# A new order for the repeating stage of an attention kernel: two first mixes together, scores late, the second mixes apart

## The chip, the cores and the metric

One core of a Trainium2 chip runs one program. The metric is the time of one execution on the device in microseconds (us). Five engines work beside each other, each through its own instructions in order: TensorE (PE in the profile, with its weight loads as PEld), VectorE (DVE), ScalarE (ACT), GpSimd (POOL), and SyncE (SP), which here issues the DMA transfers.

## The reference

Three parts follow each other: an attention whose heads are mixed before and after the softmax, an ELU layer, and a layer of eight experts with routing. The change lies in the first part alone. With batch 4, 12 heads, 448 positions and head width 64:

```python
scores = (1 / sqrt(64)) * q @ k.transpose(0, 1, 3, 2)
scores = einsum('bhij,hg->bgij', scores, w_pre)        # first mix
scores = scores - max(scores, axis=-1, keepdims=True)
attn = exp(scores)
attn = attn / (sum(attn, axis=-1, keepdims=True) + 1e-09)
attn = einsum('bhij,hg->bgij', attn, w_post)           # second mix
out = attn @ v                                         # values
# then: ELU layer (1792x768 by 768x2048 and back), and the experts
```

## The kernel before, in words

The queries of a batch are cut into four tiles: three of 120 rows and one of 88. A tile's scores are computed for all heads, laid out anew by DMA so that 10 rows by 12 heads fill the partitions, mixed, put through the softmax, mixed again and multiplied with the values. A block is 10 query rows (the last two of an 88-row tile are 4 rows), a pair is two blocks, and a unit is two pairs; the last unit of an 88-row tile has one pair. There are 16 tiles of three units, so 48 **periods**, `for n in range(NP)`. A period works on four things at once, in a software pipeline written out by hand:

- the **first mix** (`mix_pre`, tile `c`, L200) of the pairs of unit n: 8 products of 64 rows by 64 columns on TensorE a pair; then maxima (`top`, DVE L208), exponentials with their sums (`softmax`, ACT L217), reciprocals (`norm`, DVE L224 and L225) and the scaled mixing weights `kr` (POOL L229);
- the **second mix** (`mix_post`, tile `f`, L243) of the pairs of unit n-1: 64 products, 64 by 64, into two PSUM buffers, which are all there are of this kind (`ps_f`, 2), and two copies out of them into `at` (L248);
- the **scores** (`qk`, L159) of a unit five periods ahead: 12 products of 64 rows by 120 (or 88) columns, and copies to `s` on ACT (L163) and DVE (L164); their queries are split into a high part (ACT L146) and a low part (DVE L147), and at the start of a batch the keys likewise (ACT L138, POOL L139);
- the **values** (`av`, tile `xp`, L264) of a tile whose second mix is finished: 24 products of 128 rows by 64 columns and 8 of 64 by 64, a copy (DVE L273) and a store.

SP issues the new layout (`relayout`, L192), the loads and the stores, in program order. In the last five periods `next(mix)` puts pieces of the ELU layer's preparation between these steps, at four places of a period.

The order of the body is the order of the calls. Before the change it is: first mix of pair 0, second mix of old pair 0, first mix of pair 1, second mix of old pair 1, scores, values. A second mix is followed at once by one copy on ACT and one on DVE. `ps_w`, five buffers, holds the results of first mixes and scores.

Of the kernel before, what the change touches and what calls it, by code (L numbers as in the profile page):

```python
# [8 lines left out]
FP32 = mybir.dt.float32  # L9
# [3 lines left out]
ACTF = mybir.ActivationFunctionType  # L13
ALU = mybir.AluOpType
# [4 lines left out]
B, H, S, D = 4, 12, 448, 64  # L19
# [57 lines left out]
def attention(tc, q, k, v, w_pre, w_post, xT, mix):  # L77
# [12 lines left out]
    with ExitStack() as ctx, ExitStack() as mixing, ExitStack() as scoring:  # L90
        pool = lambda name, bufs, ctx=ctx, **kw: ctx.enter_context(tc.tile_pool(name=name, bufs=bufs, **kw))
        at_p = pool("a_at", 2)
        e_p = pool("a_e", 6)
        st_p = pool("a_st", 4)
        const = pool("a_const", 1)
        v_p = pool("a_v", 1)
# [44 lines left out]
        def split_q(T, u):  # L141

            n = ROWS[tiles[T][1]][1]
            t = qt[T, u] = q_p.tile([128, 2, 2, 120], FP32R, tag="q", name="qq")
            raw = raw_q[T][:, 2 * u:2 * u + 2, :n]
            nc.scalar.copy(out=t[:, 0, :, :n], in_=raw)  # L146
            nc.vector.tensor_tensor(out=t[:, 1, :, :n], in0=raw, in1=t[:, 0, :, :n], op=ALU.subtract)  # L147

        def qk(T, p):

# [24 lines left out]
        dr, cs, tops, sms, es, ks = {}, {}, {}, {}, {}, {}  # L175

        d_all = [d_p.tile([128, S], FP32, name=f"d{i}") for i in range(ND)]
        n_d = [0]
# [16 lines left out]
        def mix_pre(U):  # L195
            pss = [ps_w.tile([128, 512], FP32, tag="w", name="c") for _ in range(2)]
            d = dr.pop(U)
            for j in range(2):
                for z, ps in enumerate(pss):
                    nc.tensor.matmul(out=ps[j * UP:(j + 1) * UP, :S], lhsT=kpre_up[UP:UP + HP, :] if z else kpre_low,  # L200
                                     rhs=d[z, j])
            cs[U] = [ps[:, :S] for ps in pss]

        def top(U):
            tops[U] = []
            for c in cs[U]:
                t = st_p.tile([128, 1], FP32, tag="nmx", name="nmx")
                nc.vector.tensor_reduce(out=t, in_=c, op=ALU.max, axis=AX.X, negate=True)  # L208
                tops[U].append(t)

        def softmax(U):

            sms[U] = st_p.tile([128, 2], FP32, tag="sm", name="sm")
            es[U] = []
            for i, (c, t) in enumerate(zip(cs.pop(U), tops.pop(U))):
                e = e_p.tile([128, S], FP32, tag="e", name="e")
                nc.scalar.activation(out=e, in_=c, func=ACTF.Exp, bias=t, accum_out=sms[U][:, i:i + 1])  # L217
                es[U].append(e)

        def norm(U):  # L220

            sm = sms.pop(U)
            rs = st_p.tile([128, 2], FP32, tag="rs", name="rs")
            nc.vector.tensor_scalar(out=rs, in0=sm, scalar1=1e-9, scalar2=None, op0=ALU.add)  # L224
            nc.vector.reciprocal(out=rs, in_=rs)  # L225
            ks[U] = []
            for i in range(2):
                kr = e_p.tile([128, HP], FP32, tag="kr", name="kr")
                nc.gpsimd.tensor_scalar(out=kr, in0=kposts[i], scalar1=rs[:, i:i + 1], scalar2=None, op0=ALU.mult)  # L229
                ks[U].append(kr)  # L230

        def mix_post(U):

# [127 lines left out]
        for n in range(NP):  # L361
            cur, old = units[n], units[n - 1] if n else ()
            new = units[n + 1] if n + 1 < NP else ()
            T, u = when(n + 5)
            T1, u1 = when(n + 6)
            T2, u2 = when(n + 7)
            for U in new[1:]:
                relayout(U)
            store()
            if n == NP - 5:  # L370
                scoring.close()
            late = n >= NP - 5
# [11 lines left out]
            for i in range(2):  # L384
# [12 lines left out]
                if i == 0:  # L397
                    softmax(cur[i])
                if i == 1 and T < len(tiles):
                    scores = [qk(T, 2 * u), qk(T, 2 * u + 1)]  # L400
                if late:
                    next(mix)
            norm(cur[0])
            for f in scores:
                f()
            for U in cur[1:]:
                norm(U)
            if T1 < len(tiles):
                split_q(T1, u1)
            if n >= 3:  # L410
                av(n // 3 - 1, n % 3)()
            if T1 < len(tiles) and tiles[T1][1] == 0:
                split_k(tiles[T1][0], 2 * u1, nc.gpsimd)
                split_k(tiles[T1][0], 2 * u1 + 1, nc.gpsimd)
            if late:
                next(mix)
        mixing.close()
# [893 lines left out]
```

## Time and profile before

| | us |
|---|---|
| median of 3 runs | 1040.65 (1037.43 to 1047.15) |
| the profiled execution | 1035.86 |
| its span | 1034.1 |
| attention, its steady periods (52 to 330 us of the span) | 278 |

The busy time of an engine is the union of its instructions. Starts of products on TensorE are recorded; their ends are modelled, so the distance from the start of one group to the start of the next is the better measure of a group. The row of a timeline that merges several instructions has the start of the first.

### The profile page before, as it was taken

The numbers are of one execution on the slowest core, as the hardware profiler recorded it, in microseconds if no ns is written. First come the engines' busy times: TensorE is split into PE (matmuls) and PEld (weight loads), VectorE is DVE, ScalarE is ACT, GpSimd is POOL, SyncE is SP. The second block draws the span as 40 slices with busy tenths as digits, with TensorE's granted clock in tenths as the row PEclk, the third lists the DMA queues.
The fourth block names the chain that finished last, engine by engine and source line by source line (L and its number), as shares of the span: only waits on it lengthen the run. The fifth ranks groups of instructions, "written<-read, shape, count | busy, mean of one in ns | idle before, by whom it ended". The sixth has DMA issues, their size and how long they took to land. (4 is left out here: it accounts for less than half of the span.)

```text
span 1034.1 us, 30182 instructions
## 1 busy us (share of the span) xinstructions
PE 993.6 (96%) x12226; PEld 874.0 (85%) x12226; DVE 768.2 (74%) x1589; ACT 531.8 (51%) x1077; POOL 228.3 (22%) x295
## 2 busy tenths in 40 slices
PE   7899999999999899999999999999999999899997
PEld 4577777777777688999999998999999998798987
DVE  6678788788788788767666576868686848999963
ACT  5557567567666565444544453121212107788861
POOL 2134224223322312222333200101000003312001
PEclk9899999999999999999999999999999999999999
DMA  5555566466555685545665469633343387999800
GB/s 166 198 174 145 166 217 181 150 205 192 156 185 179 179 248 190 158 163 173 222 216 194 170 211 311 205 92 123 93 122 96 99 310 264 394 395 399 340 9 34
DMA packets 134219, 199.69 MB, mean 193 GB/s; under 512 B 35860, under 2 KB 101400, under 8 KB 133821
## 3 DMA queue, kind: packets, MB, share of 16 engines
q1 hardware_dynamic: 131933, 191.27, 56.2%
q0 software_dynamic: 2144, 6.46, 1.6%
q8 instruction: 97, 1.59, 0.7%
q14 instruction: 45, 0.37, 0.1%
HBM read 122.47 MB, written 37.65 MB: 155 GB/s over the span
## 5 line engine op out<-in xcount | busy, mean ns | idle before, releaser
L855 PE MATMUL o<-w,gh 128*128 128x384 f32 (+2 forms) x1344 | 238.9, 337 | 2.2 <-ACT w L460 1.6
L855 PEld LDWEIGHTS o<-w,gh 128*128 128x128 f32 x1344 | 231.9, 188 | 5.3 <-ACT w L460 2.0
L582 PE MATMUL h<-xh,w 128*128 128x448 f32 x1152 | 234.5, 365 | 0.0
L582 PEld LDWEIGHTS h<-xh,w 128*128 128x128 f32 x1152 | 216.1, 188 | 17.6 <-issue 0.2
L243 PEld LDWEIGHTS f<-kr,e 64*64 64x64 f32 x5888 | 121.5, 137 | 51.0 <-issue 34.0
L229 POOL TENSOR_SCALAR kr<-kpost,rs 128x60 f32<-128x60 f32 x184 | 80.9, 454 | 252.4 <-DVE rs L225 227.8
L243 PE MATMUL f<-kr,e 64*64 64x60 f32 x5888 | 121.5, 223 | 9.6 <-issue 3.6
L745 DVE SCALAR_TENSOR_TENSOR junk<-x,wrow 128x768 f32<-128x768 f32 x117 | 111.8, 955 | 18.1 <-ACT x L885 12.8
L1023 DVE TENSOR_TENSOR wlo<-w1t,whi 128x1536 fp32r<-128x1536 f32 x64 | 110.9, 1751 | 14.3 <-ACT whi L1021 13.9
L208 DVE TENSOR_REDUCE nmx<-c 128x1 f32<-128x448 f32 x184 | 106.2, 619 | 19.5 <-PE c L200 19.2
L217 ACT ACTIVATE e<-c,nmx 128x448 f32<-128x448 f32 x184 | 114.4, 639 | 2.1 <-DVE nmx L208 2.1
L248 ACT COPY at<-f 128x480 f32<-128x480 f32 (+1 forms) x92 | 52.1, 566 | 114.2 <-PE f L243 114.2
L497 POOL TENSOR_TENSOR wf<-a,p 128x768 f32<-128x768 f32 x32 | 66.6, 2082 | 178.1 <-DVE p L495 141.1
L1021 ACT CAST whi<-w1t 128x1536 fp32r<-128x1536 f32 x64 | 93.9, 1482 | 20.6 <-PE ph L1050 9.9
L200 PE MATMUL c<-d,kpre_up 60*64 60x448 f32 x368 | 94.1, 565 | 1.6 <-ACT s L163 1.6
L264 PEld LDWEIGHTS xp<-at,v 128*64 128x64 f32 (+1 forms) x1536 | 74.0, 135 | 24.7 <-issue 14.1
L264 PE MATMUL xp<-at,v 128*64 128x120 f32 (+3 forms) x1536 | 91.1, 265 | 3.6 <-DVE rs L225 1.8
L200 PE MATMUL c<-d,kpre_low 64*64 64x448 f32 x368 | 91.5, 552 | 2.9 <-DMA d<-s 2.9
L159 PE MATMUL qk<-k,qq 64*120 64x448 f32 (+1 forms) x576 | 80.0, 400 | 8.1 <-ACT k L138 5.1
L730 ACT CAST gh<-gr 128x512 fp32r<-128x512 f32 x56 | 35.0, 625 | 98.7 <-PE o L855 38.8
L159 PEld LDWEIGHTS qk<-k,qq 64*120 64x120 f32 (+1 forms) x576 | 52.6, 182 | 23.5 <-ACT k L138 5.9
L248 DVE COPY at<-f 128x480 f32<-128x480 f32 (+1 forms) x92 | 58.8, 640 | 13.9 <-PE f L243 9.7
(177 smaller groups left out, 1251.8 us busy)
## 6 DMA issues: line engine op xcount, KB each, us to landing
w1t<-in_moe_w_dram SPq DMA_DIRECT2D x64, 768.0 KB
d<-s SPq DMA_DIRECT2D x176, 210.0 KB
gT<-g SPq DMA_DIRECT2D x64, 224.0 KB
f<-in_moe_w_in_dram SPq DMA_DIRECT2D x16, 768.0 KB
f<-in_moe_w_out_dram SPq DMA_DIRECT2D x16, 768.0 KB
gr<-gT SPq DMA_DIRECT2D x48, 256.0 KB
rk<-in_k_dram SPq DMA_DIRECT2D x24, 224.0 KB
xr<-xT SPq DMA_DIRECT2D x24, 224.0 KB
```

The lines of the kernel that those rows point to most:

```text
L159: nc.tensor.matmul(out=ps[:n, :S], lhsT=qt[T, p // 2][rows, a, p % 2, :n], rhs=kt[b, p][rows, z, :], start=(i == 0), stop=(i == 2))
L200: nc.tensor.matmul(out=ps[j * UP:(j + 1) * UP, :S], lhsT=kpre_up[UP:UP + HP, :] if z else kpre_low, rhs=d[z, j])
L208: nc.vector.tensor_reduce(out=t, in_=c, op=ALU.max, axis=AX.X, negate=True)
L217: nc.scalar.activation(out=e, in_=c, func=ACTF.Exp, bias=t, accum_out=sms[U][:, i:i + 1])
L243: nc.tensor.matmul(out=ps[to, c // 2, :, z, :], lhsT=e[rows, keys], rhs=kr[rows, :])
L248: copy(out=to[:, :, r + j * m:r + (j + 1) * m], in_=at[:, :, first:first + m])
L264: nc.tensor.matmul(out=ps[z * 64:(z + 1) * 64, i, :n], lhsT=t[:, z, jc % t.shape[2], :], rhs=att[T][:t.shape[0], jc, 2 * p + z, :n], start ...
L582: nc.tensor.matmul(out=ps, lhsT=w[:, a, kk, :], rhs=xs[tb, kk][:, z, :], start=(kk == 0 and a + z == 0), stop=(kk == NK - 1 and a == 1))
L745: nc.vector.scalar_tensor_tensor(out=t[:, o:o + n], in0=x2, scalar=1.0, in1=w, op0=ALU.mult, op1=ALU.mult, accum_out=lg[:, e:e + 1])
L855: mm = nc.tensor.matmul(out=po[c][:, :cols[c].stop - cols[c].start], lhsT=gs[i][fc // GC][:, a, fc % GC, :], rhs=wo[fc][:, z, cols[c]], st ...
L1021: nc.scalar.copy(out=hi, in_=t)
L1023: nc.vector.tensor_tensor(out=lo, in0=t, in1=hi, op=ALU.subtract)
```

## The change

The body of the period is written in another order: both first mixes, the second mix of old pair 0, the values (of the tile that was finished a period earlier than before, `n - 1` in place of `n`), all scores, the second mix of old pair 1. The split of the queries moves from one period ahead into the period of the scores: its high part on ACT before the first mixes' exponentials, its low part on DVE behind the four maxima. `norm` is called once for both pairs, on one tile of four sums. The two copies of the last second mix both go to ACT. The split of the keys is spread over the period, the weights' pool gets a seventh buffer, and the four `next(mix)` of a late period stand at other places.

```diff
-        e_p = pool("a_e", 6)
+        e_p = pool("a_e", 7)
...
-        def norm(U):
-
-            sm = sms.pop(U)
-            rs = st_p.tile([128, 2], FP32, tag="rs", name="rs")
...
+        def norm(Us):
+
+            k = 2 * len(Us)
+            sm = sms.pop(0)
+            es_now.clear()
+            rs = st_p.tile([128, 4], FP32, tag="rs", name="rs")
+            nc.vector.tensor_scalar(out=rs[:, :k], in0=sm[:, :k], scalar1=1e-9, scalar2=None, op0=ALU.add)
+            nc.vector.reciprocal(out=rs[:, :k], in_=rs[:, :k])
...
-            if late:
-                next(mix)
...
-            scores = []
-            for i in range(2):
-                if i < len(cur):
-                    mix_pre(cur[i])
+            if n and T < len(tiles):
+                high_q(T, u)
+            for i, U in enumerate(cur):
+                mix_pre(U)
                 if i == 0 and n + 2 < NP:
                     relayout(units[n + 2][0])
-                moves = mix_post(old[i]) if i < len(old) else []
-                if i < len(cur):
-                    top(cur[i])
-                    if i == 1:
-                        softmax(cur[i])
-                if moves:
-                    moves[1](nc.scalar.copy)
-                    moves[0](nc.vector.tensor_copy)
-                if i == 0:
-                    softmax(cur[i])
-                if i == 1 and T < len(tiles):
-                    scores = [qk(T, 2 * u), qk(T, 2 * u + 1)]
-                if late:
-                    next(mix)
-            norm(cur[0])
+            for U in cur:
+                top(U)
+            if n and T < len(tiles):
+                low_q(T, u)
+            softmax(cur[0])
+            moves, scores = [mix_post(U) for U in old[:1]], []
+            weighted = [av((n - 1) // 3 - 1, (n - 1) % 3)] if n >= 4 else []
+            if T < len(tiles):
+                scores.append(qk(T, 2 * u))
+            for U in cur[1:]:
+                softmax(U)
+            if late:
+                next(mix)
+            for m in moves:
+                m[1](nc.scalar.copy)
+                m[0](nc.vector.tensor_copy)
+            keys = T1 < len(tiles) and tiles[T1][1] == 0
+            if keys:
+                split_k(tiles[T1][0], 2 * u1, nc.gpsimd)
+            if late:
+                next(mix)
+            norm(cur)
+            for f in weighted:
+                f()
+            if T < len(tiles):
+                scores.append(qk(T, 2 * u + 1))
             for f in scores:
                 f()
-            for U in cur[1:]:
-                norm(U)
-            if T1 < len(tiles):
-                split_q(T1, u1)
-            if n >= 3:
+            if keys:
+                split_k(tiles[T1][0], 2 * u1 + 1, nc.gpsimd)
+            moves = [mix_post(U) for U in old[1:]]
+            if late:
+                next(mix)
+            for m in moves:
+                m[1](nc.scalar.copy)
+                m[0](nc.scalar.copy)
+            if n == NP - 1:
                 av(n // 3 - 1, n % 3)()
...
```

A full period on TensorE, before (`c` first mix, `f` second mix, `qk` scores, `xp` values; a second mix is 32 products in the program, 64 on the engine):

```order
L200 MATMUL c<-d_154,kpre_low 64x448
L200 MATMUL c<-d_154,kpre_up 64x448
L200 MATMUL c<-d_155,kpre_low 64x448
L200 MATMUL c<-d_155,kpre_up 64x448
L243 MATMUL f<-kr,e 64x12x5 x32
L200 MATMUL c<-d_156,kpre_low 64x448
L200 MATMUL c<-d_156,kpre_up 64x448
L200 MATMUL c<-d_157,kpre_low 64x448
L200 MATMUL c<-d_157,kpre_up 64x448
L243 MATMUL f<-kr,e 64x12x5 x32
L159 MATMUL qk<-k,qq 120x448 x12
L264 MATMUL xp<-at,v 64x120 x16
```

The same period with the change:

```order
L208 MATMUL c<-d_154,kpre_low 64x448
L208 MATMUL c<-d_154,kpre_up 64x448
L208 MATMUL c<-d_155,kpre_low 64x448
L208 MATMUL c<-d_155,kpre_up 64x448
L208 MATMUL c<-d_156,kpre_low 64x448
L208 MATMUL c<-d_156,kpre_up 64x448
L208 MATMUL c<-d_157,kpre_low 64x448
L208 MATMUL c<-d_157,kpre_up 64x448
L264 MATMUL f<-kr,e 64x12x5 x32
L285 MATMUL xp<-at,v 64x120 x16
L167 MATMUL qk<-k,qq 120x448 x12
L264 MATMUL f<-kr,e 64x12x5 x32
```

The two second mixes no longer have only a first mix between them: values and scores stand there now, and two first mixes behind the last one.

A full period on ScalarE with the change (`e` exponentials, `at` copies of the second mix, `s` copies of the scores, `qq` high part of the queries):

```order
L145 CAST qq<-rq 128x240
L229 ACTIVATE e,sm<-c,nmx 128x448 x4
L269 COPY at<-f 128x48x10
L171 ACTIVATE s<-qk 120x448 x2
L269 COPY at<-f 128x48x10 x2
```

Before, the queue had one copy `at` ahead of the four exponentials, one behind them, then the scores and last the queries' cast; now the cast is first and the two copies of the second mix stand together at the end, with the next period's cast behind them.

## Rows read from the trace of the kernel before

**Rows 1.** Windows: length, busy PE, PEld, DVE, ACT, POOL (count), granted clock, DMA, GB/s.
```profile
52.00:330.00 278.00, 270.35 (x7124) 208.03 (x7118) 222.49 (x531) 184.31 (x509) 85.30 (x169) 1.00 0.57 178
```

**Rows 2.** Waits, 52 to 330 us: who waited for whom, us, times, longest.
```profile
PEld f L243 <- issue: 26.5, 33, 1.2
...
PEld xp L264 <- issue: 13.1, 55, 0.3
...
PEld xp L264 <- ACT at L248: 4.6, 9, 0.6
```

**Rows 3.** Timeline of TensorE's products, one full period: start, us, what.
```profile
146.23 0.59 PE L200 MATMUL c<-d,kpre_up 60*64 60x448 f32 x1
...
147.03 1.24 PE L243 MATMUL f<-kr,e 64*64 64x60 f32 x63
148.05 0.54 PE L200 MATMUL c<-d,kpre_up 60*64 60x448 f32 x1
...
148.43 0.54 PE L200 MATMUL c<-d,kpre_up 60*64 60x448 f32 x1
...
149.09 1.30 PE L243 MATMUL f<-kr,e 64*64 64x60 f32 x64
150.32 1.45 PE L159 MATMUL qk<-k,qq 64*88 64x448 f32 x12
151.70 1.90 PE L264 MATMUL xp<-at,v 128*64 128x120 f32 x29
153.34 0.59 PE L200 MATMUL c<-d,kpre_up 60*64 60x448 f32 x1
...
153.44 0.27 PE L264 MATMUL xp<-at,v 64*64 64x120 f32 x2
```

**Rows 4.** Timeline of TensorE, first and last full period's first product (39 periods apart).
```profile
52.51 0.59 PE L200 MATMUL c<-d,kpre_up 60*64 60x448 f32 x1
...
330.40 0.59 PE L200 MATMUL c<-d,kpre_up 60*64 60x448 f32 x1
```

**Rows 5.** Timeline of ScalarE in the same period.
```profile
148.38 0.57 ACT L248 COPY at<-f 128x480 f32<-128x480 f32 x1 [1.71 <-PE f L243]
148.84 0.63 ACT L217 ACTIVATE e<-c,nmx 128x448 f32<-128x448 f32 x1
...
151.28 0.59 ACT L248 COPY at<-f 128x480 f32<-128x480 f32 x1
151.73 0.99 ACT L163 ACTIVATE s<-qk 88x448 f32<-88x448 f32 x2
```

**Rows 6.** Groups by form, 52 to 330 us: busy us, mean ns, idle before.
```profile
L139 POOL TENSOR_TENSOR k<-rk,k 128x448 fp32r<-128x448 f32 x18 | 20.0, 1133 | 0.0
```

**Rows 7.** Timeline of TensorE, a period behind a unit of one pair.
```profile
281.63 0.59 PE L200 MATMUL c<-d,kpre_up 60*64 60x448 f32 x1
...
286.05 0.86 PE L159 MATMUL qk<-k,qq 64*120 64x448 f32 x5 [0.19 <-ACT e L217]
286.84 1.50 PE L264 MATMUL xp<-at,v 128*64 128x88 f32 x29
288.11 0.59 PE L200 MATMUL c<-d,kpre_up 60*64 60x448 f32 x1
```

**Rows 8.** Timeline of TensorE in the last periods, without scores.
```profile
333.26 1.30 PE L243 MATMUL f<-kr,e 64*64 64x60 f32 x64
334.49 1.90 PE L264 MATMUL xp<-at,v 128*64 128x120 f32 x29
...
364.03 2.01 PE L264 MATMUL xp<-at,v 128*64 128x120 f32 x32
365.97 3.92 PE L582 MATMUL h<-xh,w 128*128 128x448 f32 x18
```

**Rows 9.** Timeline of SP and ScalarE: load of the ELU layer's first weights, its first use.
```profile
331.92 0.35 SPq L474 DMA_DIRECT2D f<-in_moe_w_in_dram  x1
...
338.24 0.89 ACT L485 ACTIVATE a<-f 128x768 f32<-128x768 f32 x1 [2.20 <-DMA d<-s]
```

More of the change, by code (lines that the diff above doesn't have):

```diff
@@ L139, in split_k, with high_q, low_q, split_q @@
             eng.tensor_tensor(out=t[:, 1], in0=raw, in1=t[:, 0], op=ALU.subtract)
-        def split_q(T, u):
+        def high_q(T, u):
             n = ROWS[tiles[T][1]][1]
             t = qt[T, u] = q_p.tile([128, 2, 2, 120], FP32R, tag="q", name="qq")
-            raw = raw_q[T][:, 2 * u:2 * u + 2, :n]
-            nc.scalar.copy(out=t[:, 0, :, :n], in_=raw)
-            nc.vector.tensor_tensor(out=t[:, 1, :, :n], in0=raw, in1=t[:, 0, :, :n], op=ALU.subtract)
+            nc.scalar.copy(out=t[:, 0, :, :n], in_=raw_q[T][:, 2 * u:2 * u + 2, :n])
+        def low_q(T, u):
+            n = ROWS[tiles[T][1]][1]
+            t = qt[T, u]
+            nc.vector.tensor_tensor(out=t[:, 1, :, :n], in0=raw_q[T][:, 2 * u:2 * u + 2, :n], in1=t[:, 0, :, :n],
+                                    op=ALU.subtract)
+        def split_q(T, u):
+            high_q(T, u)
+            low_q(T, u)
         def qk(T, p):
@@ L174, in attention @@
         NP = len(units)
-        dr, cs, tops, sms, es, ks = {}, {}, {}, {}, {}, {}
+        dr, cs, tops, sms, es, ks, es_now = {}, {}, {}, {}, {}, {}, []
         d_all = [d_p.tile([128, S], FP32, name=f"d{i}") for i in range(ND)]
@@ L209, in top, with exps, one @@
                 tops[U].append(t)
-        def softmax(U):
[L213 to L218, printed above, removed]
-        def norm(U):
-            sm = sms.pop(U)
-            rs = st_p.tile([128, 2], FP32, tag="rs", name="rs")
-            nc.vector.tensor_scalar(out=rs, in0=sm, scalar1=1e-9, scalar2=None, op0=ALU.add)
-            nc.vector.reciprocal(out=rs, in_=rs)
-            ks[U] = []
-            for i in range(2):
-                kr = e_p.tile([128, HP], FP32, tag="kr", name="kr")
-                nc.gpsimd.tensor_scalar(out=kr, in0=kposts[i], scalar1=rs[:, i:i + 1], scalar2=None, op0=ALU.mult)
-                ks[U].append(kr)
+        def exps(U):
+            if not sms:
+                sms[0] = st_p.tile([128, 4], FP32, tag="sm", name="sm")
+            k = 2 * len(es_now)
+            es[U] = []
+            es_now.append(U)
+            def one(i, c, t):
+                e = e_p.tile([128, S], FP32, tag="e", name="e")
+                nc.scalar.activation(out=e, in_=c, func=ACTF.Exp, bias=t, accum_out=sms[0][:, k + i:k + i + 1])
+                es[U].append(e)
+            return [lambda i=i, c=c, t=t: one(i, c, t) for i, (c, t) in enumerate(zip(cs.pop(U), tops.pop(U)))]
+        def softmax(U):
+            for e in exps(U):
+                e()
+        def norm(Us):
[5 more added lines that the diff above has]
+            nc.vector.reciprocal(out=rs[:, :k], in_=rs[:, :k])
+            for i, U in enumerate(Us):
+                ks[U] = []
+                for z in range(2):
+                    kr = e_p.tile([128, HP], FP32, tag="kr", name="kr")
+                    nc.gpsimd.tensor_scalar(out=kr, in0=kposts[z], scalar1=rs[:, 2 * i + z:2 * i + z + 1], scalar2=None,
+                                            op0=ALU.mult)
+                    ks[U].append(kr)
         def mix_post(U):
@@ L382, in attention @@
                     load_k(tiles[T2][0], 2 * u2 + 1)
[L383 to L386 removed]
+            if n and T < len(tiles):
+                high_q(T, u)
+            for i, U in enumerate(cur):
+                mix_pre(U)
                 if i == 0 and n + 2 < NP:
                     relayout(units[n + 2][0])
[L389 to L402 removed]
@@ L403, in attention @@
-            norm(cur[0])
+            for U in cur:
+                top(U)
+            if n and T < len(tiles):
+                low_q(T, u)
+            softmax(cur[0])
[7 more added lines that the diff above has]
+                next(mix)
```

3 lines of the change are left out of this document (removed).

## The prediction

> **What bounds the kernel now.** I read the page first, for the engine with the most busy time: TensorE, in every slice of the span. The change touches attention alone, so the next view is the table of windows for its steady part [rows 1]: TensorE 270 of 278 us, VectorE 222, ScalarE 184, and a granted clock of 1.00. So a microsecond is gained only where TensorE itself loses one. Third, the waits in that stretch [rows 2]. The largest of TensorE's loads of weights is the second mix's, 26.5 us in 33 periods, but most of it lies under products that are still running. What it costs is read from the timeline [rows 3], from start to start: first mix to second mix 0.80, back to a first mix 1.02, to the second second mix 1.04, to the scores 1.23, to the values 1.38, to the next period's first mix 1.64; 7.11 together. The 39 periods between the two products of [rows 4] take 277.9, 7.13 each, so this period is typical. A first mix by itself is two passes, 0.38 apart (148.05 to 148.43 [rows 3]), so 0.76; the 1.04 before the second second mix has 0.28 of waiting in it. ScalarE shows for what [rows 5]: the copy out of the second mix's PSUM starts at 148.38, takes 0.57 and ends at 148.95; the product that reuses the two buffers starts at 149.09. The reader is to see there 0.33 from the last product of a second mix (148.05) to the copy, and 0.14 from the copy's end to the next product.
>
> **The wait that goes: up to 0.28 a period.** With values and scores between the two second mixes (over 3 us), the first copies are long done. The wait could come back at the other end: the last second mix is followed by both ACT copies and then, two first mixes later, by the next second mix in the same buffers. The copies need 0.33 to start, 0.45 from one to the next (151.28 to 151.73 [rows 5], a copy and the instruction behind it), 0.57 for the second and 0.14 to the product: 1.49. The two first mixes cover 0.76 + 0.76 = 1.52. That is level; I count it at nothing, and 0.1 a period if the two copies don't overlap (0.57 for 0.45).
>
> **What the new order costs.** TensorE's products are the same in number. Start to start, a new period is: first mix to first mix 0.76, to the second mix 0.76, to the values 1.23 (the same sequence is in the last periods, 333.26 to 334.49 [rows 8]), values to scores X, scores to second mix 1.38 (taken from scores to values), second mix to first mix 1.02: 5.15 + X. X isn't in the trace. Before, a first mix follows the values after 1.64, and it starts at 153.34 while the values' last products, of 64 rows by 64 columns like its own, start at 153.44 [rows 3]: the two overlap. Where the values are followed by products over the whole array, it is 1.94 (364.03 to 365.97 [rows 8]). Scores take all columns, in two halves of the rows, of which the values' tail leaves one free; so X is nearer to the upper row, and I take 1.89. The period is then 7.04 against 7.11: the wait of 0.28 is gone, and 0.25 is paid for an overlap lost. [...]
>
> **Sum.** (1) Of the 39 periods, 33 have two pairs now and before: 33 x 0.07 = 2.3 us gained. (2) The values wait for the last copy `at` where a tile has just been finished: 9 loads of weights in 4.6 us, 0.5 each, against at most 0.3 for the other 55 [rows 2]; since the values come a period later, 9 x 0.2 = 1.8 us go. (3) Behind a unit of one pair a period has only one second mix, and the scores run into the first mixes' exponentials: they wait in their middle (286.05), and the period takes 6.48 [rows 7]. In the new order a second mix and the values stand between; with values of 88 rows (1.27, 0.37 less [rows 7]) it is 0.76 + 0.76 + 1.23 + 1.52 + 1.38 = 5.65: 0.83 gained, three times, 2.5 us. The period before it, of one first mix, keeps a wait of its size and counts at nothing. (4) The last five periods and the start: nothing, with bounds of 2.2 either way, the wait of ScalarE for the ELU layer's first weights [rows 9]. That load is issued by SP behind two layout transfers now, so it lands later; but the second mix of that period waits for ScalarE in either order. Together 6.6 us: a span of 1034.1 - 6.6 = 1027.5, and an execution of 1035.86 - 6.6 = 1029.3. The profiled execution is 4.8 below the median of the runs (1040.65); the same difference taken from the median gives **1034**.
>
> **What I cost at nothing, and its cover.** The query cast now stands ahead of four exponentials on ScalarE, and behind two copies: copies to 1.34 after the period's first product, cast about 0.4, so exponentials from 1.7, when the first maximum is there too. They take 2.44 (148.84 to 151.28 [rows 5]), the copy behind them ends at about 4.7, and the second mix that needs its buffer comes at 6.0. The low part of the queries comes behind four maxima at about 3.7; the scores start at about 4.6. Each tenth by which it were later than the third product would be a tenth a period. The reciprocals wait for all four exponentials: the weights `kr` are ready at about 6.5 and are wanted at 8.6, in the next period's second mix; in 9 periods the keys' subtraction on POOL, 1.13 [rows 6], goes ahead of them and leaves about 1.2. ScalarE gains one copy, 0.57, for the one that VectorE loses: 39 of them are 22 us on the 184 of [rows 1], still below TensorE's 270. SP issues the same transfers; the stores of the values come earlier in a period, the loads of new values one period later, and are still two periods ahead of their use. The first mix of the second pair starts a second mix (1.02) earlier, but its layout transfer was issued in the period before. The seventh buffer costs no time.
>
> **Rivals.** *The overlap is kept* (chance 0.31): X is 1.64, as between values and first mix, because the free half of the rows takes scores at once. The period is 6.79, 0.32 less; 33 x 0.32 + 1.8 + 3 x 1.08 = 15.6 us, **1025**. [...] *The wait comes back behind the two copies* (0.11): the level of 1.49 against 1.52 holds only if ScalarE is free when the last product ends. If the score copies, which now come just before (0.99 for two [rows 5]), or the keys' casts still run, each tenth is lost in every period, and the second mixes of all following periods are late by it. It decides from 0.17 a period, where the 6.6 are used up, and passes 1% at 0.44; with 0.5, 39 x 0.47 - 6.6 = 11.7 us slower, **1052**. Against it: the scores end about 1.0 us before the last second mix does, and only half of the 0.99 is left to do then. *The last periods get worse* (0.08): the ELU layer's first cast is late by another 2.2 on ScalarE and the maxima queued behind its partner on VectorE with it, up to 4 us for both: 1034 + 4 = 1038.
>
> **How the numbers follow.** My forecast has the remaining 0.50, by itself 1029 to 1040. A run of this kernel can be told from no change from about 1%, 10.4 us. Faster by over 1%: nearly all of the first rival and a tenth of the forecast, 0.33. Slower: most of the second rival and a little of the rest, 0.12. Within: 0.55. The range of 8 in 10 takes in the first rival with 2 us below it, X at 1.94, the copies that don't overlap, and the worse last periods with the spread of the runs: 1023 to 1046.
>
> **What would show it.** In the changed kernel's timeline: first mix to first mix 0.76; values to scores between 1.64 and 1.94, which decides between forecast and first rival; scores to second mix about 1.38; a period of 7.0. In the waits: the second mix's 26.5 us of idle loads gone, or, by the second rival, again there behind ScalarE's `at`. The period behind a unit of one pair 5.7 instead of 6.5. I am wrong if scores to second mix costs much more or less than scores to values, or if TensorE waits for maxima or `kr`.

## The result, and the profile after

The changed kernel takes 1027.57 us (median; 1023.39 to 1030.95) against 1040.1 for the kernel before, a ratio of 0.9855 with a 95% interval of 0.981 to 0.990. Run again beside other kernels it was 1030.92 against 1041.3, 10.4 us less, 0.9868 (0.9823 to 0.9913). So it is faster by 1.3 to 1.5%. The forecast of 1034 (0.6%) was half of that; 1027.57 lies inside the range, near the value of the first rival, but not for that rival's reason.

The profiled execution of the changed kernel is 1030.95, the slowest of its four; that of before, 1035.86, was one of the faster. So the two profiles differ by 4.9 us where the medians differ by 12.5. The time is sought in the distances between groups first, and in the ends of the parts second.

The windows of the same stretch, which answer to [rows 1] (length, busy PE, PEld, DVE, ACT, POOL, clock, DMA, GB/s), the waits of TensorE there, which answer to [rows 2], and the first products of the first and last full period, which answer to [rows 4]:

```profile
52.00:330.00 278.00, 270.66 (x7300) 206.95 (x7293) 193.31 (x431) 215.79 (x558) 83.21 (x172) 0.99 0.59 180
```

```profile
PEld f L264 <- issue: 17.9, 54, 1.2
...
PEld f L264 <- POOL kr L249: 7.3, 23, 0.3
...
PEld f L264 <- ACT at L269: 0.6, 3, 0.2
```

```profile
50.75 0.54 PE L208 MATMUL c<-d,kpre_low 64*64 64x448 f32 x1
...
322.80 0.54 PE L208 MATMUL c<-d,kpre_low 64*64 64x448 f32 x1
```

TensorE is as busy as before, 270.66 of 278 us; it only does more in them. The values' wait for `at` (4.6 us in 9) is gone. Loads of the second mix's weights are still idle for 17.9 us, and for 7.3 more behind `kr`, but that lies under running products: the distance from the scores to a second mix is 1.37 to 1.42 whichever of the two labels its load has. Three loads wait for ScalarE's copies, 0.6 us in all, each in the period of a unit with one pair. Between the two products of the third block lie 272.05 us, 5.84 less than before.

One full period on TensorE (start, duration, operation), which answers to [rows 3]:

```profile
148.64 0.54 PE L208 MATMUL c<-d,kpre_low 64*64 64x448 f32 x1
...
150.15 1.14 PE L264 MATMUL f<-kr,e 64*64 64x60 f32 x64
151.22 2.01 PE L285 MATMUL xp<-at,v 128*64 128x120 f32 x32
153.16 1.45 PE L167 MATMUL qk<-k,qq 64*88 64x448 f32 x12
154.54 1.16 PE L264 MATMUL f<-kr,e 64*64 64x60 f32 x64
155.52 0.54 PE L208 MATMUL c<-d,kpre_low 64*64 64x448 f32 x1
```

Start to start: both first mixes 1.51, second mix to values 1.07 (1.04 is the median of 39), values to scores 1.94, scores to second mix 1.38, back to a first mix 0.98; 6.88 here, 6.86 from the medians. ScalarE at the turn of this period, which answers to [rows 5]:

```profile
148.88 1.03 ACT L269 COPY at<-f 128x480 f32<-128x480 f32 x2 [0.58 <-PE f L264]
```

The two copies end at 149.91, and the product that wants their PSUM starts at 150.15. The period behind a unit of one pair, which answers to [rows 7], is 5.90 from first mix to first mix, where it was 6.48:

```profile
108.43 0.54 PE L208 MATMUL c<-d,kpre_low 64*64 64x448 f32 x1
...
109.94 1.11 PE L264 MATMUL f<-kr,e 64*64 64x60 f32 x64
110.98 2.01 PE L285 MATMUL xp<-at,v 128*64 128x120 f32 x32
112.92 1.48 PE L167 MATMUL qk<-k,qq 64*120 64x448 f32 x12
114.33 0.59 PE L208 MATMUL c<-d,kpre_low 64*64 64x448 f32 x1
```

At the end, the row of [rows 8] that closes attention (the first `h` at 365.97) is at 360.40, and the ELU layer's first cast of [rows 9] comes at 332.83 in place of 338.24:

```profile
332.83 0.89 ACT L516 ACTIVATE a<-f 128x768 f32<-128x768 f32 x1 [2.84 <-issue]
...
360.40 1.89 PE L613 MATMUL h<-xh,w 128*128 128x448 f32 x8
```

What is behind attention takes 661 to 670 us on TensorE in the fourteen profiles read for this; two profiles of one kernel differ by 2 to 3 us. A single profile can't weigh a few us there, so only attention is compared below.

### The profile page after: what moved, and what is told of

It is laid out like the page before. It is cut to its first block, busy times and chain, and to the rows that moved or that the text cites. A ratio compares the mean times of both kernels' runs of the same rounds, so it can differ in the third digit from the quotient of the medians.

```text
span 1029.2 us, 30044 instructions
## 1 busy us (share of the span) xinstructions
PE 990.3 (96%) x12226; PEld 869.2 (84%) x12226; DVE 728.8 (71%) x1457; ACT 563.4 (55%) x1121; POOL 226.9 (22%) x295
## 5 line engine op out<-in xcount | busy, mean ns | idle before, releaser
L264 PEld LDWEIGHTS f<-kr,e 64*64 64x64 f32 x5888 | 109.2, 137 | 40.2 <-issue 25.0
L216 DVE TENSOR_REDUCE nmx<-c 128x1 f32<-128x448 f32 x184 | 102.6, 617 | 54.3 <-PE c L208 54.3
L249 POOL TENSOR_SCALAR kr<-kpost,rs 128x60 f32<-128x60 f32 x184 | 78.5, 449 | 210.0 <-DVE rs L244 146.8
L264 PE MATMUL f<-kr,e 64*64 64x60 f32 x5888 | 111.5, 222 | 7.0 <-ACT at L269 3.4
L269 ACT COPY at<-f 128x480 f32<-128x480 f32 (+1 forms) x136 | 72.2, 565 | 29.0 <-PE f L264 28.1
L208 PE MATMUL c<-d,kpre_low 64*64 64x448 f32 x368 | 84.7, 555 | 1.6 <-DMA d<-s 1.6
L208 PE MATMUL c<-d,kpre_up 60*64 60x448 f32 x368 | 83.3, 558 | 2.3 <-ACT s L171 2.3
L171 ACT ACTIVATE s<-qk 120x448 f32<-120x448 f32 (+1 forms) x96 | 51.8, 543 | 43.5 <-PE qk L167 34.5
L172 DVE TENSOR_SCALAR s<-qk 120x448 f32<-120x448 f32 (+1 forms) x96 | 58.6, 622 | 21.6 <-PE qk L167 15.0
```

The costliest lines, as they stand in the source:

```text
L249: nc.gpsimd.tensor_scalar(out=kr, in0=kposts[z], scalar1=rs[:, 2 * i + z:2 * i + z + 1], scalar2=None, op0=ALU.mult)
L264: nc.tensor.matmul(out=ps[to, c // 2, :, z, :], lhsT=e[rows, keys], rhs=kr[rows, :])
```

## A loss that was in no term: stops of TensorE

Four rows of TensorE's timeline in the changed kernel (the bracket has the idle time in front and what ended it; "issue" is nothing that the profile shows), and the windows around them (the last columns are the granted clock, DMA share and GB/s):

```profile
171.80 0.43 PE L285 MATMUL xp<-at,v 128*64 128x120 f32 x4
174.44 1.88 PE L285 MATMUL xp<-at,v 128*64 128x120 f32 x28 [2.21 <-issue]
176.25 2.60 PE L167 MATMUL qk<-k,qq 64*120 64x448 f32 x12
178.78 1.44 PE L264 MATMUL f<-kr,e 64*64 64x60 f32 x64
```

```profile
165.00:170.00 5.00, 5.00 (x117) 3.86 (x120) 3.42 (x9) 4.68 (x13) 2.29 (x4) 1.00 0.70 188
...
174.00:176.00 2.00, 1.56 (x28) 1.40 (x28) 0.07 (x1) 0.04 (x1) 1.64 (x4) 1.00 0.42 101
176.00:178.00 2.00, 2.00 (x16) 1.55 (x14) 0.61 (x2) 0.24 (x1) 0.00 (x0) 0.51 0.23 27
178.00:180.00 2.00, 2.00 (x68) 1.44 (x67) 1.05 (x2) 0.85 (x2) 0.00 (x0) 0.64 0.39 89
```

TensorE stops in the middle of the values for 2.21 us, and in the window from 176 us the granted clock is 0.51, in the next 0.64: the scores, 1.38 to the second mix elsewhere, take 2.53. The period that began at 169.25 lasts 10.80, 3.94 more than its neighbours.

Between 52 us and the end of attention the changed kernel has 8 stops of over 0.25 us with that label, 8.4 us together (10 and 8.0 in its second profile); the kernel before has 3, 3.6 us. If all of TensorE's records (matmuls, weight loads and its few semaphore instructions) are counted in the order of their starts, all 8 of the changed kernel stand at the same remainder: 1218, 3265, 5314, 7618, 8386, 9666, 11970, 16066, that is 193 or 194 above a multiple of 256. Those of before do too (2241, 9922, 16066), and so do all 85 such stops of the fourteen profiles. The table of DMA queues has this row:

```profile
q8 instruction: 97, 1.59, 0.6%
```

These are 97 packets of 16 KB, and TensorE's 24,664 records are 96.3 times 256. At each of the 8 stops the last of these packets landed 1.3 to 1.6 us before TensorE went on. So the stops have one fixed place in every 256 records, and there are about as many packets as blocks of 256; that TensorE waits there for its next 256 instructions is the author's reading of these counts, which no run shows directly. What makes it stop at one such place and not at the next is not in the trace.

## The experiments

The experiments share a table: median distances in us from the start of one group to the start of the next, in the full periods between 52 and 325 us, in the order of each kernel (`c` first mix, `f` second mix, `xp` values, `qk` scores; `cc` two first mixes).

| kernel | distances | ratio to before (95%) |
|---|---|---|
| before | c→f 0.80, f→c 1.02, c→f 1.04, f→qk 1.23, qk→xp 1.41, xp→c 1.64 | 1 |
| changed | cc→f 1.51, f→xp 1.04, xp→qk 1.94, qk→f 1.40, f→c 0.98 | 0.9868 (0.9823, 0.9913) |
| values first (before) | c→f 0.80, f→c 0.93, c→f 1.06, f→xp 1.34, xp→qk 1.94, qk→c 1.41 | 1.0113 (1.0066, 1.0161) |
| small products first | cc→f 1.51, f→xp 0.93, xp→qk 1.90, qk→f 1.41, f→c 0.98 | 0.9826 (0.9777, 0.9874) |
| scores last | cc→f 1.55, f→xp 1.12, xp→f 1.64, f→qk 1.22, qk→c 1.41 | 0.9966 (0.9936, 0.9996) |
| scores in the middle | cc→f 1.51, f→qk 1.08, qk→xp 2.02, xp→f 1.64, f→c 1.07 | 1.0019 (0.9990, 1.0049) |
| cast between copies | cc→f 1.51, f→xp 1.19, xp→qk 1.94, qk→f 1.41, f→c 0.98 | 0.9937 (0.9909, 0.9964) |

**The changed kernel again**, for a second profile.

> The changed kernel as it is, beside the next three. Theory: 12 to 15 us below the kernel before, of which the steady periods give 0.25 to 0.27 each (33 x 0.26 = 8.6), the waits of the values 1.9 and the periods behind a one-pair unit 2.2. In the profile: two first mixes 1.51, second mix to values 1.04, values to scores 1.94, scores to second mix 1.4, second mix to first mix 0.98. The stalls of TensorE whose releaser the profile calls issue (8.4 us in the first profile, 3.6 in that of the kernel before) should lie at other places and have another sum if they are chance, the same places if they belong to the order.

Measured: 1030.92 us, 10.4 below before where 12 to 15 were expected; the distances as in the first profile to 0.01. Some stops are at other places, but those at counts 5314, 7618, 9666 and 16066 come again. So they belong partly to the order of the program and partly to chance.

**One part alone: the values a period later**, in the kernel before.

> The kernel before with one part of the change: the values of a tile one period later. Theory: only the wait of the values' loads for the last copy goes, 9 x 0.2 = 1.8 us, and the order of a period stays at 7.11; 0.2% faster, not told from none. Rival, that the lag is the bulk of the gain: 8 us or more faster.

```diff
-            if n >= 3:
+            if n >= 4:
+                av((n - 1) // 3 - 1, (n - 1) % 3)()
+            if n == NP - 1:
                 av(n // 3 - 1, n % 3)()
```

Measured: 1040.08 against 1041.3, 0.9968 (0.9939 to 0.9996): about 3 us of gain with 0.4 to 6 in the interval, the distances those of before. The term of 1.8 is compatible with it, and in its profile no load of the values waits for `at` any more. The lag also has a price: behind a unit of one pair the values are now of 120 rows and not of 88, and that period takes 6.86 where it took 6.48. The lag alone is not the change's gain.

**Values ahead of the scores, in the kernel before**, with the lag and the old order of the mixes.

> The kernel before with the lag and the values ahead of the scores: first mix, second mix, first mix, second mix, values, scores. The wait for the copies stays. Theory: what the order costs is seen alone: second mix to values 1.23 (a second mix that has waited), values to scores 1.94, scores to first mix 1.4, then 0.76, 0.98, 1.04: 7.35 in place of 7.12, 33 x 0.23 - 1.8 = 6 us slower than the kernel before. Rival, that the overlap of values and first mix is worth nothing: 2 us faster.

```diff
...
+                if i == 1 and n >= 4:
+                    weighted = [av((n - 1) // 3 - 1, (n - 1) % 3)]
                 if i == 1 and T < len(tiles):
                     scores = [qk(T, 2 * u), qk(T, 2 * u + 1)]
...
-            for f in scores:
+            for f in weighted + scores:
                 f()
...
```

Measured: 1056.96, 12 us slower than before by the ratio, twice the 6 that were expected (the interval has 7 to 17). The distances of the table add up to 7.48, those of before to 7.14. The rows of one period, the wait of its second mix as the profile puts it (loads, us, times, longest), and the two copies that free its buffers:

```profile
148.41 1.14 PE L243 MATMUL f<-kr,e 64*64 64x60 f32 x61
149.34 0.54 PE L200 MATMUL c<-d,kpre_low 64*64 64x448 f32 x1
...
150.40 0.70 PE L243 MATMUL f<-kr,e 64*64 64x60 f32 x22
```

```profile
PEld f L243 <- POOL kr L229: 25.5, 32, 0.9
```

```profile
149.69 0.57 ACT L248 COPY at<-f 128x480 f32<-128x480 f32 x1 [1.21 <-PE f L243]
149.88 0.65 DVE L248 COPY at<-f 128x480 f32<-128x480 f32 x1
```

The name `kr` misleads: these had been ready for 0.65 us or more when the second second mix started. It starts 0.145 behind the end of ScalarE's copy, in all 34 cases, as it does in before (1.06 behind its first mix in place of 0.76). Behind that wait it needs mostly 1.25 to 1.35 to the values; why it needs more than 1.04 is shown below, under the prediction. The distance of 1.94 from values to scores is here too. Without their stops, the 39 periods are 12.2 us longer than those of before without theirs: the distances alone give the 12 us. The stops of this profile (9.4 us against 1.4 in the same periods) would come on top, 20 us in all, which lies outside the interval of the ratio.

**The values' 8 small products (64 by 64) ahead of their 24 large ones**, in the changed kernel.

> The changed kernel with the values' 8 products of 64 rows by 64 columns ahead of the 24 of 128 by 64, so that they follow the second mix in its own form and can overlap its end. Theory, that each change of form on TensorE costs about 0.1 and that what has the same form overlaps: one change less a period, and the overlap of 0.2: second mix to scores from 2.98 to between 2.70 and 2.88, 4 to 11 us below the changed kernel. Rival, that the values cost the same wherever the small products stand: no change against the changed kernel.

```diff
-            for js in (range(JC - 1), (JC - 1,)):
+            for js in ((JC - 1,), range(JC - 1)):
...
```

```profile
160.22 1.11 PE L264 MATMUL f<-kr,e 64*64 64x60 f32 x64
161.15 1.97 PE L285 MATMUL xp<-at,v 64*64 64x120 f32 x32
163.05 1.49 PE L167 MATMUL qk<-k,qq 64*120 64x448 f32 x12
```

Second mix to scores is 2.83 and was 2.98; the period is 6.73. The small products have the form of the second mix's (64 by 64), so one of four changes of form in a period is gone. 1025.8 us, the lowest median of all, 5 below the changed kernel in the same series; the intervals of the two ratios overlap.

**Where the copies and the query split stand.** In the first kernel one of the two last copies goes on VectorE, in the second the split is one period ahead, as before the change.

> Of the period's last second mix the second copy out of PSUM goes on VectorE and not on ScalarE. Theory (the cover of the copies holds, 1.49 us of copies against about 1.52 us of scores and first mixes): the copies end nothing, so no stretch of the period changes by more than 0.03 us and the time is that of the changed kernel, within 3 us. Rival (two copies on one ScalarE hold the next second mix's PSUM now and then): the distance from the last first mix to the second mix falls and with it the period, by up to 0.1 us in 30 periods, so 2 to 4 us faster. Other rival (VectorE is in the way of the maxima): the first mixes' maxima come later, the second mix waits, 5 us slower or more.

```diff
-                m[0](nc.scalar.copy)
+                m[0](nc.vector.tensor_copy)
```

> The query split goes back to the end of the period ahead of the one that needs it, as before the change; all else of the change stays. Theory (the split is beside TensorE's work in both places, the order alone gives the gain): period 6.86 us as in the changed kernel, time within 3 us of it. Rival (the split ahead of the maxima delays the exponentials and with them the second mix): the second mix starts 0.2 to 0.5 us later in periods that split, so 30 periods by 0.3 us are 5 to 15 us slower than the changed kernel.

```diff
-            if n and T < len(tiles):
-                high_q(T, u)
...
-            if n and T < len(tiles):
-                low_q(T, u)
...
+            if T1 < len(tiles):
+                split_q(T1, u1)
             if keys:
```

Measured: 1030.22 (0.9875, 0.9838 to 0.9912) and 1030.76 (0.9891, 0.9852 to 0.9929), with every distance of the table equal to the changed kernel's to 0.01. Neither part bears on the time by more than the runs can tell: the gain is the order on TensorE. One difference lies outside the table, in the three periods of a unit with one pair, where a single first mix stands between the two last copies and the next second mix. First the changed kernel, then the one with the copy on VectorE:

```profile
102.65 1.52 PE L264 MATMUL f<-kr,e 64*64 64x60 f32 x64
104.10 2.01 PE L285 MATMUL xp<-at,v 128*64 128x120 f32 x32
```

```profile
100.71 1.16 PE L264 MATMUL f<-kr,e 64*64 64x60 f32 x64
101.80 2.01 PE L285 MATMUL xp<-at,v 128*64 128x120 f32 x32
```

Second mix to values is 1.45 there, and 1.09 with the copies on two engines; the period is 6.74 against 6.40. So the wait does come back where the cover is one first mix, about 1 us in all.

**The cover of the copies, taken away.**

> The changed kernel with the queries' cast (0.4 us on ScalarE) between the two copies of the last second mix, so that the second copy ends 0.4 later and the next second mix has to wait for its PSUM: 1.49 + 0.40 = 1.89 us of copies against 1.52 us of first mixes. Theory (a second mix that had to wait runs slower, 17 ns from product to product and not 14.6): first mix to second mix 1.85 to 1.95 and second mix to values 1.20 to 1.25, so the period is 6.86 + 0.37 + 0.17 = 7.4, and 33 periods by 0.54 are 18 us slower than the changed kernel, about 1047. First rival (the distance of 1.04 belongs to the place between first mixes and values): first mix to second mix 1.9, second mix to values 1.04, period 7.23, 12 us slower. Second rival (the copies do not hold the second mix, the cover is larger than 1.52): all distances as in the changed kernel, time within 3 us of it.

```diff
-            if n and T < len(tiles):
-                high_q(T, u)
...
             for m in moves:
                 m[1](nc.scalar.copy)
+            if T1 < len(tiles):
+                high_q(T1, u1)
+            for m in moves:
                 m[0](nc.scalar.copy)
```

ScalarE and TensorE at the turn of a period:

```profile
148.94 0.57 ACT L269 COPY at<-f 128x480 f32<-128x480 f32 x1 [0.64 <-PE f L264]
149.40 0.34 ACT L145 CAST qq<-rq 128x176 fp32r<-128x176 f32 x1
149.64 0.57 ACT L269 COPY at<-f 128x480 f32<-128x480 f32 x1
```

```profile
150.15 1.26 PE L264 MATMUL f<-kr,e 64*64 64x60 f32 x64
151.35 2.01 PE L285 MATMUL xp<-at,v 128*64 128x120 f32 x32
```

The cast cost 0.24 and not 0.40, since it overlaps the copy ahead of it: the second copy ends at 150.21. The second mix starts at 150.15 as in the changed kernel, on the buffer that is free; its third product, the first that waits for the other buffer, starts at 150.264, 0.054 behind the end of that copy, and the values 1.19 behind the second mix in place of 1.04. The price is 0.15 in 33 periods, 5 us; the ratio rose by 0.007, 7 us, from 0.9868 to 0.9937, with intervals that just touch. All three expectations missed the size. The theory of slower products is wrong: from 150.37 on they come four in 58 ns, exactly as in the changed kernel. Of the 0.15, 0.10 are the wait for the second buffer inside the group; 0.05 are lost at the start besides.

**Two other orders.** In the first the scores stand at the end, behind the last second mix; the second pair's exponentials move behind the first copies, and one of the last copies to VectorE. In the second the scores stand ahead of the values.

> The changed kernel with the values between the two second mixes, and the scores all at the end: first mix, first mix, second mix, values, second mix, scores. Theory (a group of 64x64 or 128x64 products that ends in one form and is followed by the same form saves the cost of the form's change, and a second mix that follows running products takes 1.04 us and not 1.23): the period is 6.64 to 6.83 us against 6.86, so 1 to 7 us faster than the changed kernel. Rival (the exponentials of the second pair come later than the values end, so the other second mix waits): period 7.0 us or more, 5 us slower or more than the changed kernel.

```diff
...
-            if T < len(tiles):
-                scores.append(qk(T, 2 * u))
...
             moves = [mix_post(U) for U in old[1:]]
+            if T < len(tiles):
+                scores.append(qk(T, 2 * u))
...
+            if T < len(tiles):
+                scores.append(qk(T, 2 * u + 1))
...
```

1037.64 us, a period of 6.94, some 10 us slower than the changed kernel by the ratios. The theory fell, and the rival's wait isn't there either. The form changes four times in a period, as in the changed kernel (into the large values, into their small products, into the scores, into the first mix); second mix to scores is 1.22, about the most that the expected period leaves for it, and the first two distances are 0.04 and 0.08 longer than in the changed kernel. The longer period gives 33 x 0.08 = 2.6 of the 10 us; where the rest lies is not shown.

> The changed kernel with the scores ahead of the values (first mix, first mix, second mix, scores, values, second mix), the query split one period ahead and one of the last two copies on VectorE, so that the exponentials start earlier and free the first mixes' PSUM for the scores. Theory (a period is the sum of distances that depend only on the form of the groups on both sides): 1.51 for the first mixes, 1.06 for a second mix that did not wait, 1.38 from scores to values, 1.64 from values to a group of the same form, 0.98 from second mix to first mix, together 6.57 us against 6.86, so 33 x 0.29 = 9.6 us faster than the changed kernel, about 1021. Rival (the scores wait for buffers that the exponentials still read): the scores take 0.3 to 0.8 longer, period 6.9 to 7.4, 0 to 18 us slower than the changed kernel.

```diff
+            if T < len(tiles):
+                scores += [qk(T, 2 * u), qk(T, 2 * u + 1)]
             weighted = [av((n - 1) // 3 - 1, (n - 1) % 3)] if n >= 4 else []
...
```

```profile
154.51 1.15 PE L264 MATMUL f<-kr,e 64*64 64x60 f32 x64
155.59 1.05 PE L167 MATMUL qk<-k,qq 64*88 64x448 f32 x7
156.83 0.84 PE L167 MATMUL qk<-k,qq 64*88 64x448 f32 x5 [0.18 <-ACT e L229]
157.59 1.90 PE L285 MATMUL xp<-at,v 128*64 128x120 f32 x29
159.24 0.26 PE L264 MATMUL f<-kr,e 64*64 64x60 f32 x1
159.24 0.26 PE L285 MATMUL xp<-at,v 64*64 64x120 f32 x1
```

```profile
PEld qk L167 <- ACT e L229: 15.3, 39, 0.6
```

1041.7 us. Three of the five distances came out as summed (1.51, 1.08 for 1.06, 1.64). Second mix to first mix is 1.07 and not 0.98, and scores to values 2.02 and not 1.38, because the scores wait for PSUM that the exponentials still read. That is the named rival. The values between second mix and scores are thus what gives the exponentials their time in the changed order.

**The stops, shifted.** One second mix of the second period runs twice, so that 128 more instructions stand ahead of all that follows; the second kernel has the small products first as well.

> The changed kernel with the 64 products of one second mix at the start of attention (second period, ahead of a wait for data) run twice: 128 more instructions of TensorE, half of 256. Theory (the unexplained stops of TensorE stand at every 256th instruction of its stream, where a new packet of 16 KB of instructions has to land): the stops stand at the same counts, 194 above a multiple of 256, and so at other places of the program than in the changed kernel (not in the values at 172 to 174 us, which follow 128 instructions earlier in the block); the distances between groups stay the same; the sum of the stops is 3 to 10 us, the time 1026 to 1034. Rival (the stops belong to what the program does there): the stops are at the same places of the program, the values at 172 to 174 us and at 333 us, and the count above a multiple of 256 is 66.

```diff
-            moves = [mix_post(U) for U in old[1:]]
+            moves = [mix_post(U, 2 if n == 1 else 1) for U in old[1:]]
```

> The changed kernel with the values' 8 small products first and the same 128 instructions more. Theory (the gain of the values' order and the stops are independent): the period stays 6.73 us, the stops move by half a block, and the time differs from that of the values' order alone, 1025.8, by the difference of the sums of stops, at most 4 us either way. Rival (the gain of the values' order was a smaller sum of stops): 1029 to 1032, as the changed kernel.

Two rows of TensorE in the first of the two kernels:

```profile
163.69 2.01 PE L285 MATMUL xp<-at,v 128*64 128x120 f32 x31 [1.59 <-issue]
...
331.77 1.98 PE L264 MATMUL f<-kr,e 64*64 64x60 f32 x64 [5.54 <-ACT at L269]
```

The stops stand at counts 5826, 7361, 17090 and 17345, again 193 or 194 above a multiple of 256, and so at other products: the longest is again in the values, but a period earlier, and the one of 1.5 to 2 us that stood at 333 to 334 us is gone. Nothing is gained there: a wait for ScalarE stands in its place, 5.54 us (second row), where the changed kernel has a stop of 1.97 and then 2.46 of that wait. Of the rival nothing is left. The sum of the stops fell to 3.5 us, and in the profile attention ends at 355.16, against 360.40 and 362.02. The time did not follow: 1029.13, 0.9885 (0.9858 to 0.9911), no lower than the changed kernel. With the small products first, 1026.16 (0.9864, 0.9834 to 0.9895), with the same distances as without the shift. In the profiled execution itself, 1033.62 us, what attention gained is lost behind it: from its end to the end of the span it takes 676.7 us, where the two profiles of the changed kernel have 668.8 and 670.4. Whether that belongs to the shift, and whether the stops are as long in executions without a profile, the runs don't say.

**A second profile of before.**

> The kernel before, unchanged, for a second profile. Theory (idle time of TensorE that no wait explains falls partly at places fixed by the order and partly by chance): the sum of these gaps between 52 us and the end of attention is 2 to 8 us and most of them stand at other places than in the first profile, while the distances between groups in the period are the same to 0.02 us. Rival (the order of the work before leaves fewer such gaps than the change does): 3 to 4 us again, at the same places.

3.3 us of stops, at the same three counts as in the first profile of before, so here the rival was right: the order of before has few stops, three in each profile, and at fixed places.

## Why the prediction was half right

*What bounds the kernel* held: TensorE is busy nearly all the time in both (270.35 and 270.66 of 278 us), and the gain came out of its order. Of the two edits on other engines that were tried apart, the query split cost nothing, and the copy about 1 us, in the periods with one first mix.

*The wait that goes* held in place and was mis-sized. The first copies are hidden, and the last two, level by the sum (1.49 against 1.52), are covered in every period of two pairs. But the wait was priced by its first product alone, 0.28, and the rest of it stood in another term. The step that failed is "to the second mix 0.76, to the values 1.23": **1.23 was read in [rows 8], like the 1.23 to the scores in [rows 3], behind a second mix that had waited, and it holds the second half of that wait.** Without a wait it is 1.04. A second mix writes two buffers; its third product is the first that waits for the copy out of the second one. [rows 5] has ScalarE's copy, which ends at 148.95. The other copy of the same second mix is VectorE's:

```profile
148.53 0.65 DVE L248 COPY at<-f 128x480 f32<-128x480 f32 x1
```

It ends at 149.18, and the third product starts at 149.235, 0.144 behind the first product. The same holds elsewhere (medians of such second mixes without a stop, us; in all of these the values start with their large products):

| second mix | third product behind the end of the later copy | third product behind the first | second mix to the next group |
|---|---|---|---|
| changed, two pairs | long done | 0.013 | 1.04 |
| before, second one of a period | 0.055 | 0.143 | 1.23 |
| values first, second one | 0.055 | 0.258 | 1.34 |
| cast between copies | 0.053 | 0.111 | 1.19 |
| changed, unit of one pair | 0.053 | 0.371 | 1.45 |
| copy on VectorE, unit of one pair | (only the first product waits) | 0.014 | 1.09 |

Each of the last five is 1.04, plus what the third product is later than 0.013, plus 0.05 to 0.06. So in before the wait cost 0.28 + 0.13 + 0.06 = 0.47. Where the 0.05 to 0.06 come from, lost once by every second mix that had to wait, is not shown.

*X* was taken as 1.89 and measures 1.94, the same as from values to products over the whole array in [rows 8]. The 0.05 that the forecast took off for the free half of the rows was the author's estimate, and no run shows it. The values' small products first, with one change of form less, take 0.15 off second mix to scores. The first rival, X = 1.64, fell; the 1.64 is found only where the values' tail is followed by products of its own form, as in before and in the two other orders. That the measured time lies near this rival's 1025 is luck: its gain per period was to come out of X.

The sum of a period is thus 7.04 - 0.19 + 0.05 - 0.04 (second mix to first mix 0.98 for 1.02) = 6.86, so **term (1) is 33 x 0.25 = 8.3 us and not 2.3**. Term (2), 1.8, is borne out by the wait that is gone, and compatible with the lag alone. Term (3) is 3 x (6.48 - 5.90) = 1.7, not 2.5: second mix to values is 1.04 for 1.23, but with the lag the values there are of 120 rows, so values to scores is 1.94 and not 1.52. The period ahead of it was to keep "a wait of its size" and was counted at nothing; it fell from 7.14 to 6.74, 3 x 0.4 = 1.2. Its two second mixes stood back to back before, with 0.82 of idle time between them; now one first mix stands between the copies and the next second mix, and the wait is shorter. Together 13.0 us, close to the 12.5 between the medians (10.4 in the second series).

The profile shows 5.84 of them in these 39 periods. The stops take most of the rest: 6.4 us of gaps in the changed kernel's against 1.4, and 1.7 more for the period in which the clock fell (10.80 less 6.86 less 2.21). No term of the prediction had them, and no row of before pointed to them but the "issue" of [rows 2].

*The last periods* cancel in the first profiles: the first full period begins 1.76 earlier, since the values of one unit moved out of the start, and from 322.80 to the end of attention it is 37.60 against 35.57 before, with those values. In the second profiles it is 39.78 against 36.74. The second rival occurred only where one first mix is the cover. The third rival's mechanism occurred. The second mix behind the ELU layer's first cast, first in before and then in the changed kernel:

```profile
340.14 0.75 PE L243 MATMUL f<-kr,e 64*64 64x60 f32 x17 [2.20 <-issue]
```

```profile
338.11 1.98 PE L264 MATMUL f<-kr,e 64*64 64x60 f32 x64 [2.46 <-ACT at L269]
```

In the changed kernel the maxima wait on VectorE behind the partner of that cast (it starts at 333.75, they at 334.22), the exponentials behind the maxima (334.94), and the copy `at` behind the exponentials (337.39). With the stop ahead of it (1.97) TensorE stands idle for 4.4 us there, 5.4 in the second profile, and 5.1 to 5.6 in the variants that have no stop at this place. Before has a stop of 2.2 there and no such wait. Shorter waits elsewhere make up for it in the first profiles: from the last full period to the end of attention TensorE is idle for 5.2 us in both, in the second ones for 7.4 against 5.1. So the price is 0 to 2.3 us, inside the 4 that the prediction gave it.

## What to carry to other kernels

When an order is summed from distances, take each distance from a place where the group ahead of it started as it will in the new order: a group that waited carries the rest of its wait along, here 0.19 of 1.23 us, beside the 0.28 that stand in front of it. Where a wait is for several buffers, look for the copy that ends last, on whichever engine; in before it was VectorE's, 0.23 us behind ScalarE's. Try groups of one form next to each other, down to the order within a group, and count the changes of form in a period: here one change less took 0.15 us off second mix to scores. And what stands between two groups may be there for another engine: with the scores right behind the second mix a period was 6.57 us as summed from distances on TensorE and 7.32 as measured, with 15.3 us of waits for the exponentials at 39 of the scores' weight loads.

## What the runs showed of the hardware

- From one group to the next took 0.11 to 0.30 us more in these two cases where the form changed than where it did not: values to first mix or second mix (same form as their tail) 1.64, to scores 1.94; second mix to values 1.04, to values with their small products first 0.93. With these first, second mix to scores is 2.83 and not 2.98.
- A second mix whose buffer was still being copied started 0.145 us behind the end of the copy (all 36 cases of before, all 34 of the values first); where only its second buffer was late, the product for that one started 0.053 to 0.055 behind the end of its copy.
- Products of two groups of the same form started mixed with each other: with the scores in the middle, a second mix's first product and the values' last ones both start at 159.24. In the timeline of before, a first mix's product (153.34) starts ahead of the values' last two (153.44) [rows 3], though the program has it behind them.
- TensorE stopped for 0.3 to 2.3 us at a time, always at the same place in 256 of its records (85 of 85 stops in the fourteen profiles, 193 or 194 above a multiple). The stop of 2.21 us that ends at 174.44 is followed by a granted clock of 0.51 and 0.64 in the windows up to 180.00.
